# Four heads on separate row and column groups of TensorE, query chunks outermost, in a gated mix of full and dilated attention

## The chip, the cores and the metric

One core of one Trainium2 chip. The metric is the device time of one execution in microseconds (us). The engines are TensorE (PE in the profile; its weight loads are PEld), VectorE (DVE), ScalarE (ACT), GpSimd (POOL) and the DMA queues. Each run is called fast or slow; slow here means more than 1.5% above the fastest run of the same kernel. A burst below is a group of two or three matmuls that start together; a step is the time from one exponential of the main loop to the next.

## The reference, cut to what matters

```python
# B=1, S=2048, D=640, H=32 heads of Dh=20, bf16
g = sigmoid((x * gate_w).sum(-1))
# A: full attention
q, k, v = split(x @ A_wqkv)
a = softmax(q k^T * 20**-0.5) v  @ A_wo            # 32 heads, 2048 x 2048 scores each
# B: each position looks at 8 positions, 2 apart, backwards
b = softmax(q . k[pos - 2w], w = 0..7) v  @ B_wo
return g * a + (1 - g) * b
```

The exponentials of branch A alone are 32 x 2048 x 2048 elements. Spread over 128 partitions that is 1,048,576 columns for ScalarE, whatever the kernel looks like.

## The kernel before

Heads are taken in quads: four heads, each padded to 32 rows, fill 128 partitions. To keep the heads apart, the query tile `qz` is zero outside the rows of one head, and a score matmul contracts all 128 rows. In the value matmul the stationary operand holds the values of all four heads (128 columns), and only one head's rows of the result are used. The loop runs quad, pair, query chunk, key block: 1024 steps.

```python
def mk_qk(s):                       # two heads hh: 128 rows, 20 of them not zero
    for hh in range(2):
        ins = e.matmul(stile[i2][:, hh * 512:(hh + 1) * 512],
                       kTq[bi][:, kb * P:(kb + 1) * P], qz[zb][hh][:, :], start=True, stop=True)
def mk_exp(s):                      # 1024 columns
    e.activation(ebuf[i3][:, :], stile[i2][:, :], ACTF.Exp, scale=SCALE)
def mk_pv(s):                       # all four heads' values, one head's result is used
    for hh in range(2):
        ins = e.matmul(obank[hh][:, :], vAq[bi][:, kb, :],
                       ebuf[i3][:, hh * 512:(hh + 1) * 512], start=(kb == 0), stop=(kb == KBN - 1))
...
for s in range(nsteps):             # 1024 steps
    mk_exp(s); mk_qk(s + 2); mk_pv(s)
    run_side(s, ...)                # projections, branch B, output: one or two matmuls a step
```

Branch B multiplies values by weights and adds them up on VectorE in fp32 (`tmpB`, `blkacc`). Partial outputs of two quads are added to what already lies in HBM: they are read back (`accin`) and written again.

## Time and profile before

| | |
|---|---|
| time | 1508.4 us (median of 4; 1507.1 to 1513.6) |
| TensorE / ScalarE / VectorE busy | 84% / 69% / 55% |
| mean granted TensorE clock | 0.966 |
| exponentials waiting for score tiles | 360.7 us |

The first lines are from the page of the kernel before: busy us by engine (share of the span, instructions), the TensorE clock in 40 slices (tenths of full speed), and the chain of waits by engine.

```profile
PE 1262.1 (84%) x6402; PEld 570.6 (38%) x6528; DVE 832.1 (55%) x1707; ACT 1042.0 (69%) x1037; POOL 98.3 (7%) x176
PEclk8899999999999999998999999989999999999997
PE 67%; DVE 25%; issue 4%; DMA 3%; ACT 1%; another core or an unknown queue 0%; POOL 0%; DVEq 0%; POOLq 0%; ACTq 0%; SPq 0%
```

The page's groups of instructions follow: line, engine, operation, output<-inputs, shapes, count | busy us, mean ns of one | idle time before them and what ended it.

```profile
L598 ACT ACTIVATE ebuf<-stile 128x1024 bf16<-128x1024 f32 x1024 | 1030.8, 1023 | 384.8 <-PE stile L587 360.7
L609 PE MATMUL obank<-ebuf,vAq 128*128 128x512 bf16 x2005 | 610.6, 385 | 53.0 <-DVE rg L634 50.7
L587 PE MATMUL stile<-qz,kTq 128*128 128x512 bf16 x1985 | 608.3, 386 | 7.6 <-ACT ebuf L598 2.6
L871 DVE TENSOR_TENSOR blkacc<-blkacc,tmpB 128x640 f32<-128x640 f32 x112 | 92.4, 825 | 3.8
```

ScalarE's idle time is nearly all spent waiting for score tiles. The timeline of TensorE shows what those wait for (start in us, length, engine, line, operation, count):

```profile
102.28 0.59 PE L609 MATMUL obank<-ebuf,vAq 128*128 128x512 bf16 x2
102.71 0.38 PE L381 MATMUL side<-xT,WkP 128*128 128x512 bf16 x1
102.93 0.59 PE L587 MATMUL stile<-qz,kTq 128*128 128x512 bf16 x2
103.36 0.59 PE L609 MATMUL obank<-ebuf,vAq 128*128 128x512 bf16 x2
```

Read the starts, not the lengths: the lengths overlap. Value matmuls start at 102.28 and again at 103.36, 1.08 us later, with five matmuls in between: 0.216 us each. So a 512-column matmul takes 0.216 us of TensorE at full clock. With two side matmuls a step is 1.30 us. The kernel is bound by the number of matmuls, and most of what each streams is padding.

The 32-row matmul `side<-ones,E` uses another tile mode (32 rows instead of 128):

```profile
105.52 0.59 PE L609 MATMUL obank<-ebuf,vAq 128*128 128x512 bf16 x2
106.05 0.39 PE L381 MATMUL side<-ones,E 32*128 32x512 bf16 x1
106.36 0.11 PEld L587 LDWEIGHTS stile<-qz,kTq 128*128 128x128 bf16 x2 [0.23 <-issue]
```

The second value matmul started at 105.73; the 32-row matmul starts 0.31 us later instead of 0.216, and the next full one again 0.31 us after that. In this trace a change of tile mode costs about 0.1 us.

### The profile page before, as it was taken

How to read it: one execution, taken by the hardware profiler on the slowest of the kernel's cores; microseconds unless marked ns; L12 is line 12 of the kernel's file. 1: busy time of each engine (PE TensorE's matmuls, PEld its weight loads, DVE VectorE, ACT ScalarE, POOL GpSimd, SP SyncE). 2: the span in 40 equal slices, each digit the busy share in tenths (PEclk: the TensorE clock that was granted, in tenths of full speed). 3: DMA queues.
4: the chain of work that ended last, by engine and by line, in shares of the span. 5: the costliest groups of instructions: out<-in, count | busy, mean ns of one | idle time of the engine just before them, and what ended most of it. 6: DMA issues, size and time to landing. Idle time of an engine off the chain costs nothing.

```text
span 1507.6 us, 18855 instructions
## 1 busy us (share of the span) xinstructions
PE 1262.1 (84%) x6402; PEld 570.6 (38%) x6528; DVE 832.1 (55%) x1707; ACT 1042.0 (69%) x1037; POOL 98.3 (7%) x176
## 2 busy tenths in 40 slices
PE   3899988778788988887998889878889888987885
PEld 2444444333333444343443334334334433442332
DVE  7534344578844445688534343448883333456882
ACT  1487786657676787776877668558777656887870
POOL 5111000000100000000000010000000000000012
PEclk8899999999999999998999999989999999999997
DMA  5001000000111000000011111000010111000012
GB/s 204 24 21 38 9 13 10 9 12 13 41 39 33 13 12 15 8 11 12 21 44 36 29 45 32 11 6 14 12 44 24 38 42 42 15 11 12 16 55 74
DMA packets 24588, 43.77 MB, mean 29 GB/s; under 512 B 6929, under 2 KB 14929, under 8 KB 24496
## 3 DMA queue, kind: packets, MB, share of 16 engines
q1 hardware_dynamic: 15376, 17.64, 4.9%
q0 software_dynamic: 7808, 23.28, 4.6%
q10 hardware_dynamic: 1312, 1.64, 0.3%
q8 instruction: 55, 0.90, 0.3%
q14 instruction: 37, 0.30, 0.1%
HBM read 17.04 MB, written 10.49 MB: 18 GB/s over the span
## 4 chain that ended last, share of the span: by engine, by line
PE 67%; DVE 25%; issue 4%; DMA 3%; ACT 1%; another core or an unknown queue 0%; POOL 0%; DVEq 0%; POOLq 0%; ACTq 0%; SPq 0%
PE obank L609 24%; PE stile L587 23%; PE side L381 13%; DVE rg L634 3%; PE side L784 3%; DVE rg L632 3%; DVE tmpB L869 3%; DVE blkacc L871 2%; PE side L464 1%; DMA out_dram<-outsb 1%; PE side L849 1%; DVE oT L639 1%; DVE outsb L693 1%; DVE qTq L450 1%; DVE ident L307 1%
## 5 line engine op out<-in xcount | busy, mean ns | idle before, releaser
L598 ACT ACTIVATE ebuf<-stile 128x1024 bf16<-128x1024 f32 x1024 | 1030.8, 1023 | 384.8 <-PE stile L587 360.7
L609 PE MATMUL obank<-ebuf,vAq 128*128 128x512 bf16 x2005 | 610.6, 385 | 53.0 <-DVE rg L634 50.7
L587 PE MATMUL stile<-qz,kTq 128*128 128x512 bf16 x1985 | 608.3, 386 | 7.6 <-ACT ebuf L598 2.6
L609 PEld LDWEIGHTS obank<-ebuf,vAq 128*128 128x128 bf16 x2048 | 199.5, 99 | 311.8 <-issue 47.4
L587 PEld LDWEIGHTS stile<-qz,kTq 128*128 128x128 bf16 x2048 | 187.2, 99 | 175.4 <-PE stile L587 34.9
L702 POOL DMA_DIRECT2D out_dram<-outsb x64 | 34.7, 543 | 1309.3 <-DVE outsb L693 885.0
L779 DVE TENSOR_TENSOR prod<-qB,kB 128x256 bf16<-128x256 bf16 x320 | 77.2, 286 | 58.6 <-PE side L784 57.3
L784 PE MATMUL side<-prod,Sel 128*128 128x256 bf16 x320 | 71.3, 283 | 42.5 <-DVE prod L779 42.3
L381 PE MATMUL side<-woA_r,oTn 128*128 128x512 bf16 (+1 forms) x252 | 66.2, 309 | 45.6 <-DVE outsb L693 13.0
L632 DVE STREAM_TRANSPOSE rg<-obank 32x512 f32<-32x512 f32 x64 | 45.4, 709 | 97.6 <-PE obank L609 97.2
L871 DVE TENSOR_TENSOR blkacc<-blkacc,tmpB 128x640 f32<-128x640 f32 x112 | 92.4, 825 | 3.8
L693 DVE TENSOR_TENSOR outsb<-side,accin 128x512 bf16<-128x512 f32 x96 | 45.8, 488 | 86.4 <-PE side L381 78.3
L869 DVE TENSOR_TENSOR tmpB<-vB,attnT 128x640 f32<-128x640 bf16 x112 | 91.7, 819 | 1.9
L381 PE MATMUL side<-xT,WqkB 128*128 128x512 bf16 x189 | 72.0, 381 | 10.0 <-DVE qtmp L439 2.9
L419 DVE CAST kTq<-side 128x512 bf16<-128x512 f32 x32 | 22.1, 691 | 89.7 <-PE side L381 89.7
L784 PEld LDWEIGHTS side<-prod,Sel 128*128 128x128 bf16 x320 | 31.6, 100 | 93.5 <-DVE prod L779 60.3
L381 PE MATMUL side<-xT,WqP 128*128 128x512 bf16 x158 | 60.4, 385 | 4.7 <-DVE outsb L697 1.9
L381 PE MATMUL side<-xT,WkP 128*128 128x512 bf16 x159 | 59.7, 393 | 3.3 <-DVE WkP L410 2.9
L381 PEld LDWEIGHTS side<-woA_r,oTn 128*128 128x128 bf16 x256 | 22.9, 98 | 86.7 <-PE side L381 31.7
L646 DVE TENSOR_TENSOR oTn<-oT,Rb 64x512 bf16<-64x512 f32 x64 | 43.6, 682 | 14.1 <-DMA Rb<-oT 13.2
L464 PEld LDWEIGHTS side<-WvA,xT 128*128 128x128 bf16 x640 | 38.5, 103 | 32.6 <-PE stile L587 6.4
L849 PE MATMUL side<-ident,rep 128*128 128x128 bf16 x128 | 22.1, 248 | 32.8 <-DVE rep L844 32.7
(97 smaller groups left out, 818.4 us busy)
## 6 DMA issues: line engine op xcount, KB each, us to landing
out_dram<-outsb POOLq DMA_DIRECT2D x64, 160.0 KB, 2.1
Rb<-oT SPq DMA_DIRECT2D x64, 128.0 KB
accin<-out_dram POOLq DMA_DIRECT2D x48, 160.0 KB, 2.9
qz<-qTq SPq DMA_DIRECT2D x126, 32.0 KB, 1.8
qz<-zbuf SPq DMA_DIRECT2D x60, 32.0 KB, 1.8
WqkA<-in_A_wqkv_dram SPq DMA_DIRECT2D x1, 1600.0 KB, 15.2
WqkB<-in_B_wqkv_dram POOLq DMA_DIRECT2D x1, 1600.0 KB, 7.4
x_tm<-in_A_x_dram SPq DMA_DIRECT2D x1, 960.0 KB
```

What stands on the lines that cost most here:

```text
L381: ins = e.matmul(o, l, r, start=(k == 0), stop=(k == n - 1))
L464: ins = e.matmul(side[sbk][:, i_ * 80:i_ * 80 + 80], xT[:, c, kb * P:(kb + 1) * P], WvA[:, c, 80 * q:80 * q + 80], start=(c == 0), stop=(c ...
L587: ins = e.matmul(stile[i2][:, hh * 512:(hh + 1) * 512], kTq[bi][:, kb * P:(kb + 1) * P], qz[zb][hh][:, :], start=True, stop=True)
L598: return T("act", lambda e: e.activation(ebuf[i3][:, :], stile[i2][:, :], ACTF.Exp, scale=SCALE), reads=[("stile", i2)], writes=[("ebuf", ...
L609: ins = e.matmul(obank[hh][:, :], vAq[bi][:, kb, :], ebuf[i3][:, hh * 512:(hh + 1) * 512], start=(kb == 0), stop=(kb == KBN - 1))
L632: T("dve", lambda e: e.transpose(rg32[32 * sA:32 * sA + 32, :], obank[0][32 * sA:32 * sA + 32, :]), reads=[("obank", 0)], writes=["rgA"])
L634: T("dve", lambda e: e.transpose(rg32[32 * sB:32 * sB + 32, :], obank[1][32 * sB:32 * sB + 32, :]), reads=[("obank", 1)], writes=["rgB"])
L693: T("dve", lambda e, ob=ob, sbk=sbk, c0=c0, c1=c1, r=r: e.tensor_tensor(ob[:, c0:c1], side[sbk][:, 0:c1 - c0], accin[:, r, c0:c1], ALU.add ...
L779: T("dve", lambda e, r=r, f=f, u=u, off=off: e.tensor_tensor(prod[r][:, :], qB[:, f, u * 256:(u + 1) * 256], kB[:, f, off:off + 256], ALU. ...
L784: return e.matmul(side[sbk][:, col:col + 256], Sel4[:, wp, f, :], prod[r][:, :], start=(wp == 0 and f == 0), stop=(wp == 3 and f == CN - 1))
L869: T("dve", lambda e, vv=vv, av=av: e.tensor_tensor(tmpB[:, :, :], vv, av, ALU.mult), reads=[("attnT", ai), "vB4"], writes=["tmpB"])
L871: T("dve", lambda e: e.tensor_tensor(blkacc[:, :, :], blkacc[:, :, :], tmpB[:, :, :], ALU.add), reads=["tmpB"], writes=["blkacc"])
```

## The change

The intent: let the four heads of a quad run side by side. A score matmul takes 32 rows of one head, and four heads sit on four row groups. A value matmul has 21 columns (a column of ones for the denominator, and 20 values) on one of four column groups. Query chunks become the outermost loop, so the output of a chunk is complete and written once; keys and values of all quads stay on chip; branch B is rebuilt so that its sums over the window run on TensorE, with heads along the partitions. The input is transposed by the DMA. A static list scheduler with a cost model now decides where side work goes. The core of the diff (the file is nearly rewritten; the rest is cut):

```diff
-            for hh in range(2):
-                ins = e.matmul(stile[i2][:, hh * 512:(hh + 1) * 512],
-                               kTq[bi][:, kb * P:(kb + 1) * P], qz[zb][hh][:, :], start=True, stop=True)
+            for i in range(n):                        # n = 3, 2, 3, 2, ... units of 512 columns
+                g, r = divmod(u0 + i, 64)
+                kb, j = divmod(r, 4)                  # four heads j of one key block in turn
+                ins = e.matmul(sc[:, i * 512:(i + 1) * 512], kT[32 * j:32 * j + 32, q, kb * P:(kb + 1) * P],
+                               qT[g % 3][32 * j:32 * j + 32, :], start=True, stop=True)
...
-                ins = e.matmul(obank[hh][:, :], vAq[bi][:, kb, :], ebuf[i3][:, hh * 512:(hh + 1) * 512], ...)
+                ins = e.matmul(obank[32 * j:32 * j + DV, :], vA[:, kb, g % NQ, j, :],
+                               ebuf[s % NE][:, i * 512:(i + 1) * 512], start=(kb == 0), stop=(kb == KBN - 1), ...)
...
+        T("pe", 0.26, fn, ...)                        # cost model: a score burst
+    actc = lambda n: 0.18 + n * 0.8334e-3             # cost model: an exponential of n columns
...
+        lim = exps[s - 1].end ...                     # side work may fill TensorE up to here
+        run_side(lim)
```

## The prediction

> **What bounds it now.** TensorE's issue slots. In the timeline from 100 to 107 us every step has two score matmuls, two value matmuls and one side matmul, 0.216 us apart: 1.08 us a step; with two side matmuls, 1.30 us. The page has PE 84% busy and gives it 67% of the chain of waits; the exponentials (ScalarE) sat idle 360.7 us behind the score tiles. Steps average 1.374 us x 1024 = 1407 us, between a first exponential at 61 us and a last at 1467 us. Zero padding wastes the array: 20 of 128 rows are useful in a score matmul.
>
> **What the change does.**
> - Scores: 2048 units of 32 rows, 3 or 2 at once on separate row groups. Values: the same units on separate column groups. 4096 slots (885 us) become two short bursts in each of 820 steps. [...]
> - Cost added: tile-mode switches. [...]around the 32-row matmul side<-ones the next start comes 0.31 us later, not 0.216, on entry and exit: 0.095 us each. Three a step (rows, columns, full) x 820 = about 235 us.
> - Side matmuls: about 1270 slots of 512 columns (projections, dilated branch, output folded once), 275-285 us.
> - PE estimate: [...]about 955 us.
> - Exponentials: the same columns in 820 instructions of 1536 or 1024. Back to back the trace shows starts 0.920 us apart for 1024 columns (0.853 + 0.067), so 874 + 820 x 0.067 = 929 us, plus about 7 us of gate and dilated exponentials. This is the loop's new floor.
> - Removed: the read-back of partial outputs (48 loads), DMA fills of qz and Rb, fp32 accumulation on DVE (blkacc, tmpB: 184 us). DVE falls from 832 to about 430-500 us, off the path.
>
> **Critical path.** ScalarE and TensorE come out nearly equal. The order is static, from a cost model with exponentials 0.11 us too slow[...]. Where side work is dense (projections, dilated branch, at the start of each query chunk) a step should be PE-bound at 1.3-1.5 us; where it has run out, exponential-bound at 1.13 us. I expect a loop of about 1040 us, a first exponential at about 45 us, and a tail of about 22 us.
>
> **Predicted: 1108 us, 8 in 10 between 1035 and 1200.** Faster by over 2%: 0.97; within: 0.02; slower: 0.01.
>
> **Right or wrong.** Right if: exponentials are 85-92% busy and lead the chain, idle mostly behind the score tiles, in dense stretches; score matmuls of one burst start within some 30 ns of each other, and likewise value matmuls; gaps of about 0.1 us follow each change of shape; accin, tmpB, blkacc are gone; DVE under 500 us.
>
> **What would make it wrong.** Column tiles that don't overlap: + 0.3 us a step, total about 1250. [...] PE waiting in order on DVE's evacuations: + 50 to 100 us. Transposing loads slow: first exponential at 70 us or later. The other way, side work spread so evenly that exponentials are never starved: about 1010 us.

TensorE's sum came to about 955 us. What is measured: 0.095 us for a change of tile mode, three times a step, and 275 to 285 us of side matmuls. The total of 1108 us is the sum of the parts: a first exponential at 45 us, a loop of 1040 us and a tail of 22 us. The 0.853 us in the exponentials' floor are 1024 columns at 0.833 ns; in the trace of the changed kernel, 512 columns more take 0.427 us more from start to start (1.330 against 0.903 us), 0.834 ns a column.

## The result, and the profile after

The changed kernel takes 1118.4 us (median of 4 runs, 1110.2 to 1125.1) against 1508.4 us. The ratio is 0.740 (95% interval 0.736 to 0.744). The ratios and intervals here are made from the fast runs of both kernels in the same rounds; they differ from the ratios of the medians by up to 0.003.

The same three lines of the page, of the changed kernel:

```profile
PE 1006.9 (90%) x6213; PEld 306.2 (27%) x6213; DVE 439.5 (39%) x772; ACT 960.8 (86%) x833; POOL 35.7 (3%) x26
PEclk9599998888898989977969997988568998976657
PE 63%; ACT 20%; issue 8%; DVE 6%; ACTq 2%; DMA 1%; DVEq 0%
```

and its groups:

```profile
L743 ACT ACTIVATE ebuf<-score 128x1536 bf16<-128x1536 f32 (+1 forms) x819 | 955.3, 1253 | 98.7 <-PE score L730 93.6
L730 PE MATMUL score<-qT,kT 32*128 32x512 bf16 x2048 | 372.3, 444 | 50.4 <-ACT ebuf L743 45.3
L754 PE MATMUL obank<-ebuf,vA 128*21 128x512 bf16 x2048 | 361.4, 443 | 9.5 <-DVE vA L430 8.8
```

Idle time in front of the exponentials fell from 384.8 to 98.7 us, and the loop now sits near what ScalarE needs. VectorE fell from 832 to 440 us. But the clock line has changed as well: TensorE was granted 0.847 of full speed on average, with whole slices at 5 and 6 tenths, where before it was 0.966. And the chain of waits still leads through TensorE.

The timeline of TensorE at full clock:

```profile
600.26 0.82 PE L368 MATMUL side<-woA_r,oTn 128*128 128x512 bf16 x3
601.01 0.39 PE L730 MATMUL score<-qT,kT 32*128 32x512 bf16 x3
601.33 0.39 PE L754 MATMUL obank<-ebuf,vA 128*21 128x512 bf16 x3
601.66 0.39 PE L368 MATMUL side<-woA_r,oTn 128*128 128x512 bf16 x1
601.98 0.39 PE L730 MATMUL score<-qT,kT 32*128 32x512 bf16 x2
```

Three score matmuls (x3) have the same length as one, 0.39 us: read singly in the trace, they mostly start 3 to 4 ns apart. From the start of a burst to the next tile mode it takes 0.32 us, which is one matmul (0.216) and one change of tile mode (0.10). A step without side work is thus 0.63 us of TensorE, one with side work 0.73 us and the side matmuls.

The same two bursts near the end of the kernel, where no side work is left:

```profile
1069.79 0.61 PE L730 MATMUL score<-qT,kT 32*128 32x512 bf16 x3
1070.33 0.61 PE L754 MATMUL obank<-ebuf,vA 128*21 128x512 bf16 x3
1070.87 0.60 PE L730 MATMUL score<-qT,kT 32*128 32x512 bf16 x2
```

Now it is 0.54 us from burst to burst: matmuls of 512 columns start 0.427 us apart at half clock, and the change of tile mode adds about 0.11 us. The table by stretches (busy us and count of each engine, then the clock) shows the clock at 0.50 in one stretch and 1.00 in one 20 us later:

```profile
500.00:510.00 10.00, 9.90 (x48) 1.82 (x47) 9.51 (x15) 10.00 (x10) 0.00 (x0) 0.50 0.00 0
520.00:530.00 10.00, 9.89 (x65) 3.25 (x62) 3.39 (x8) 9.78 (x10) 0.00 (x0) 1.00 0.01 2
```

TensorE counts as 99% busy in both. The busy share says nothing here; the clock and the number of matmuls do.

**Where the loop's time goes.** Back to back, the shortest distance between two exponentials in this trace is 1.330 us after 1536 columns and 0.903 us after 1024. All 819 at that pace take 914.6 us; that is the loop's floor. I took every exponential's distance to the next above that floor, and sorted it by what TensorE did between the two score bursts, and by its clock at the first of them:

```
steps of the changed kernel      count   time above the floor
full clock, no side work          127        0.9 us
half clock, no side work          131        3.4 us
full clock, side work             465       69.2 us
half clock, side work              95       62.9 us
total                             818      136.4 us   (first exponential at 38.9 us, tail 23.8 us)
```

The tail is what comes after the last exponential. 38.9 + 914.6 + 136.4 + 23.8 = 1113.7 us, which is the span of 1113.9 us but for the last exponential's own excess. So nearly all of the loss lies in steps with side work, and nearly half of it in the 95 of them that ran at half clock. In total the clock was halved for 343 us, in pieces that are multiples of 3.41 us. (The last 1.3 us of this lie after the kernel's end; the figures of the other runs include 1 to 2 us of the same kind.)

### The profile page after: what moved, and what is told of

It is laid out like the page before. It is cut to its first block, busy times and chain, and to the rows that moved or that the text cites. A ratio compares the mean times of both kernels' runs of the same rounds, so it can differ in the third digit from the quotient of the medians.

```text
span 1113.9 us, 15049 instructions
## 1 busy us (share of the span) xinstructions
PE 1006.9 (90%) x6213; PEld 306.2 (27%) x6213; DVE 439.5 (39%) x772; ACT 960.8 (86%) x833; POOL 35.7 (3%) x26
## 4 chain that ended last, share of the span: by engine, by line
PE 63%; ACT 20%; issue 8%; DVE 6%; ACTq 2%; DMA 1%; DVEq 0%
PE side L368 25%; ACT ebuf L743 19%; PE score L730 19%; PE obank L754 18%; ACTq L290 2%; DVE stage L518 2%; DMA xT<-in_A_x_dram 1%; PE side L574 1%; PE side L528 1%; DVE vA L430 1%; DVE kT L387 1%; DVE oTt L455 1%; DVE oNt L466 1%; DVE qabs L410 0%; DVE oTn L469 0%
## 5 line engine op out<-in xcount | busy, mean ns | idle before, releaser
L743 ACT ACTIVATE ebuf<-score 128x1536 bf16<-128x1536 f32 (+1 forms) x819 | 955.3, 1253 | 98.7 <-PE score L730 93.6
L730 PE MATMUL score<-qT,kT 32*128 32x512 bf16 x2048 | 372.3, 444 | 50.4 <-ACT ebuf L743 45.3
L754 PE MATMUL obank<-ebuf,vA 128*21 128x512 bf16 x2048 | 361.4, 443 | 9.5 <-DVE vA L430 8.8
L730 PEld LDWEIGHTS score<-qT,kT 32*128 32x128 bf16 x2048 | 80.5, 93 | 318.7 <-ACT ebuf L743 211.1
L368 PE MATMUL side<-xT,kvw 128*128 128x256 bf16 (+1 forms) x760 | 142.5, 311 | 27.7 <-DMA xT<-in_A_x_dram 26.8
L754 PEld LDWEIGHTS obank<-ebuf,vA 128*21 128x21 bf16 x2048 | 75.0, 90 | 239.5 <-issue 218.2
L368 PEld LDWEIGHTS side<-xT,kvw 128*128 128x128 bf16 x760 | 63.5, 100 | 89.3 <-issue 66.9
L368 PE MATMUL side<-stage,ident 128*128 128x512 bf16 (+1 forms) x192 | 55.6, 395 | 0.0
L586 DVE TENSOR_TENSOR stage<-vB,repB 128x1280 bf16<-128x1280 bf16 x64 | 50.1, 821 | 1.1
L518 DVE TENSOR_TENSOR stage<-qB,kB 128x1280 bf16<-128x1280 bf16 x64 | 48.5, 818 | 0.2
L387 DVE TENSOR_SCALAR kT<-side,onesrow 128x512 bf16<-128x512 f32 x32 | 23.8, 743 | 39.0 <-PE side L368 39.0
```

The source lines that it names most:

```text
L368: ins = e.matmul(o, l, r, start=(first and i == 0), stop=(last and i == n - 1), skip_group_check=True)
L387: t = T("dve", dvc(512), lambda e, b=b, tcc=tcc: e.tensor_scalar(kT[:, q, tcc * 512:(tcc + 1) * 512], side[b][:, :], onesrow[:, 0:1], None ...
L518: T("dve", dvc(CN * TOK, 2), lambda e, w=w, ks=ks: e.tensor_tensor(prodB(w), qB[:, :, :], ks, ALU.mult), reads=["qB", "kB"], writes=[("pro ...
L586: T("dve", dvc(CN * TOK, 2), lambda e, w=w, vs=vs, rr=rr: e.tensor_tensor(prodB(w), vs, rr, ALU.mult), reads=["vB", ("repB", w4)], writes= ...
L730: ins = e.matmul(sc[:, i * 512:(i + 1) * 512], kT[32 * j:32 * j + 32, q, kb * P:(kb + 1) * P], qT[g % 3][32 * j:32 * j + 32, :], start=Tru ...
L743: exps[s] = T("act", actc(512 * n), lambda e: e.activation(ebuf[s % NE][:, 0:512 * n], score[s % 2][:, 0:512 * n], ACTF.Exp, scale=SCALE), ...
```

## The experiments

Theory: two separate causes hold the loop above its floor. First, the static schedule overfills steps, because its cost model knows no changes of tile mode and takes exponentials for slower than they are; TensorE then is the limit there. Second, where side work is thin, TensorE is fed so little that its clock is halved (343 us at a granted clock of 0.50), and the next side work runs at half speed (95 steps, 62.9 us above the floor). Rivals: TensorE waits for VectorE; the half clock is harmless; the gain of the change was not the side-by-side bursts at all.

All ratios in this table are against the kernel before in the same rounds. Half clock and losses are of the profiled run, which for "one more mode change" counts as slow (1227.9 us).

| run | median us | ratio | half clock us | lost: full clock + side | lost: half clock + side |
|---|---|---|---|---|---|
| the changed kernel | 1118.4 | 0.740 | 343 | 69 | 63 |
| four-group fill | 1070.4 | 0.707 | 39 | 77 | 11 |
| one-group fill | 1105.5 | 0.729 | 189 | 75 | 34 |
| one more mode change | 1211.5 | 0.797 | 527 | 87 | 140 |
| one more mode change, with fill | 1137.1 | 0.752 | 114 | 115 | 33 |
| measured costs | 1089.2 | 0.721 | 327 | 15 | 96 |
| measured costs and fill | 1064.6 | 0.703 | 105 | 19 | 51 |
| one column group (wrong result) | 1206.3 | 0.799 | 22 | 216 | 5 |
| one row group | 1980.8 | 1.312 | 1862 | 16 | 828 |
| costs, fill, relieved first group | 1015.2 | 0.672 | 22 | 21 | 1 |
| the same without the fill | 1057.1 | 0.702 | 257 | 17 | 54 |

### The changed kernel once more

> The changed kernel once more, as the base of the other runs on this chip. Expected 1110 to 1125 us and about 340 us at half TensorE clock, as before. If the half-clock time differs much while the time does not, the theory that the clock costs time is in trouble.

This was missed by a little: the median was 1128.3 us, and the profiled run (1128.6 us) was at half clock for 380 us. The four runs took 1110.6, 1128.1, 1128.6 and 1139.0 us, at mean clocks of 0.854, 0.832, 0.832 and 0.820. Only the first counts as fast, so the ratio of the first measurement is used for comparisons. Over all eight runs of this kernel the time rises as the clock falls, from 1110 us at 0.85 to 1139 us at 0.82. That already points to the clock, but it only shows that the two go together.

### Keep the clock up with zero-weight matmuls

```diff
+    def filler(s):                 # only in steps into which no side work was put
+        for j in range(4):
+            ins = e.matmul(obank[32 * j:32 * j + DV, :], zw[:, 0:DV], ebuf[s % NE][:, 0:512],
+                           start=False, stop=False, skip_group_check=True)   # zw is all zero
...
+        n0 = npe()
         run_side(lim)
+        if npe() == n0 and todo and not ended and s < NT:
+            filler(last_e)
```

> In every step without side work (about 260 of 819), four more value matmuls with zero weights, one on each column group, right after the value burst (no further change of tile mode, 0.216 us of TensorE, zeros added to the output bank; the result stays right). Theory [...] the side work that comes next then runs at half clock (63 us of lost exponential time in 95 such steps). Half-clock time falls from 343 to below 80 us and the kernel to about 1065 us (1050 to 1085). Rival: the half clock costs nothing, because those stretches wait for the exponentials: time within 10 us of the changed kernel, whatever the clock does.

It took 1070.4 us, with all four runs within 0.5 us of each other. The clock line of the four-group fill's page:

```profile
PEclk9589999999999999999999999999999999999999
```

Half-clock time fell from 343 to 39 us and the loss in half-clock side steps from 63 to 11 us. The loss at full clock did not move (69 to 77 us). Adding 263 bursts of useless matmuls (1052 matmuls) made the kernel 48 us faster by the medians; all eight runs of the changed kernel (1110 to 1139 us) lie at least 39 us above all four of this one. The rival, that the half clock is harmless, falls.

> The same fill with one column group instead of four: the same TensorE time, a quarter of the array. [...]the share in idle stretches rises only from about 0.23 to 0.28, the clock still halves for over 200 us, and the time stays above 1095 us. Rival: [...]half-clock time and kernel time equal those of the four-group fill.

The run asks what goes with the half clock: the area that is fed, or, as the rival has it, the time in which TensorE runs anything. The shares of fed area, 0.23 and 0.28, are estimates: bursts and fill of 0.216 us on their part of the array, in steps of 1.12 us (the mean of 1.330 and 0.903).

The one-group fill took 1105.5 us, with 189 us at half clock:

```profile
PEclk9699998999998889998969998998989996989758
```

It was meant to keep TensorE busy for exactly as long as the other fill. Its timeline shows that it did not always:

```profile
547.61 0.39 PE L756 MATMUL obank<-ebuf,vA 128*21 128x512 bf16 x3
547.84 0.38 PE L775 MATMUL obank<-ebuf,zw 128*21 128x512 bf16 x1
548.48 0.39 PE L756 MATMUL obank<-ebuf,vA 128*21 128x512 bf16 x2
548.49 0.39 PE L775 MATMUL obank<-ebuf,zw 128*21 128x512 bf16 x1
```

The first fill (`zw`) waits for the value burst and adds 0.216 us; the second falls on a column group that the burst left free, runs at once with it and adds nothing. That was so in 96 of 263 bursts. So this run by itself does not tell fed area from busy time. My number for the half clock (over 200 us) was slightly missed, and in runs further down the fed area does not sort the halvings (146 windows on the wrong side, where 172 fell).

### One more change of tile mode

```diff
     def fn(e):                     # the value burst
+        e.matmul(obank[:, 0:1], zw[:, :], ebuf[s0 % NE][:, 0:1], start=False, stop=False, ...)  # full array, one column
         ins = None
```

> One more change of tile mode in each step: a one-column full-array matmul with zero weights between the score burst and the value burst ([...]the result stays right). Theory: in the about 560 steps that carry side work TensorE is the limit[...]: + 55 to 80 us, about 1185 us; the steps without side work lose next to nothing. Rival: those steps are late because TensorE waits for VectorE's evacuations[...]: less than + 15 us.

It took 1211.5 us, more than expected. What one added change costs was measured in the kernel before: about 0.1 us for the change of mode, and 0.025 us from one one-column full-array matmul to the next, which together give the 0.10 to 0.13 us of the next expectation. But this run mixes two costs, because its half-clock time rose to 527 us. So the same edit was run on top of the four-group fill:

> The extra change of tile mode again, now with the four-group fill, so that the clock stays up (the first run of the extra change also raised the half-clock time from 380 to 527 us, which mixes two costs). Against the fill alone at 1070.4 us: theory, [...]about 520 steps x 0.10 to 0.13 us less what slack they have, + 35 to 65 us. Rival:[...] less than + 10 us.

The theory is that the added change lies on the path where side work is; the rival, that it hides in a wait. The run took 1137.1 us, 67 us above the fill alone, just over the expected range. Here too the excess over the floor was sorted. The steps at full clock with side work account for 38 us of that (77 to 115 us, about 0.07 us for each of some 550 steps). The rest is again clock: half-clock time rose from 39 to 114 us, most of it in the first and the last group of heads. Changes of tile mode are on the path where side work is, and the rival (TensorE waits for VectorE and the added change hides in that wait) falls: it would then have cost less than 10 us.

### Undo the concurrency

Only the order of the units in a group is changed, so that the matmuls of one burst share a row group and a column group. Instructions and counts stay the same, and the result is right. The schedule of side work stays the same but for the first 73 of 819 steps: there the new order asks for the keys and values of all key blocks early, and 36 steps carry other side work.

```diff
-                kb, j = divmod(r, 4)
+                j, kb = divmod(r, KBN)
```

> Undoes the row and column groups' concurrency and nothing else: the units of a group are taken head by head instead of four heads per key block, so that the matmuls of one burst fall on the same row group and the same column group and must run one after another. Same instructions, same counts, same schedule of side work, right result. If the concurrency is what the change gains: a burst of 2 or 3 takes 0.43 or 0.64 us instead of 0.22, a step at least 1.27 us of bursts plus about 0.44 us of side work[...], 1350 to 1450 us in all. Rival: the gain comes from the cheaper dilated branch and the dropped traffic, and bursts were never the point: below 1200 us.

One run of 1420.7 us; three more at 1454 to 1455 us, with a clock of 0.953 instead of 0.981 (the profiled one was at half clock from 32 to 158 us). The timeline of TensorE in the profiled run, in a stretch at full clock:

```profile
599.76 0.81 PE L730 MATMUL score<-qT,kT 32*128 32x512 bf16 x3
600.51 0.82 PE L754 MATMUL obank<-ebuf,vA 128*21 128x512 bf16 x3
601.26 0.39 PE L368 MATMUL side<-woBp,oB 128*128 128x512 bf16 x1
```

A burst of three is now 0.75 us to the next mode instead of 0.32. Everything else that the change brought is still in this kernel, and without the concurrency it is worth 1513.9 - 1420.7 = 93 us, 6% of the time before (median of the same rounds). Letting the bursts run side by side brings another 302 us (1420.7 - 1118.4), or 350 us against the four-group fill, whose clock was also up. Part of this is the first group of heads, where the order of side work differs as well: its steps lost 75 us in the profiled (slow) run and 26 us in the changed kernel. The rival, that the bursts were never the point, falls.

To split rows from columns, one of the two was undone at a time. For the rows, every score matmul reads head 0; for the columns, the key block picks the column group:

```diff
-  kT[32 * j:32 * j + 32, q, ...], qT[g % 3][32 * j:32 * j + 32, :]
+  kT[0:32, q, ...],               qT[g % 3][0:32, :]
```

```diff
-  obank[32 * j:32 * j + DV, :], ... start=(kb == 0), stop=(kb == KBN - 1)
+  obank[32 * (kb // 4):32 * (kb // 4) + DV, :], ... start=(kb % 4 == 0 and j == 0), stop=(kb % 4 == 3 and j == 3)
```

> Wrong result on purpose: every score matmul reads head 0 of its quad, so all fall on row group 0 and a score burst of 2 or 3 runs one after another; the value bursts stay side by side. With both undone the kernel took 1421 us in its fast run, 302 more than the changed kernel. If both halves of the concurrency are worth the same: about + 150 us, 1230 to 1310 us, less if steps have slack for one serial burst but not for two (then below 1230).

> Wrong result on purpose: the column group of a value matmul is chosen by its key block instead of its head, so that the matmuls of one value burst share a column group and run one after another; the score bursts stay side by side. Expected within 30 us of the run with one row group; if the value burst is off the path (nothing waits for it at once), clearly less.

The run with one column group took 1206.3 us, 88 us more than the changed kernel although its clock was up at 0.99, and 136 us more than the four-group fill, whose clock was also up (0.98):

```profile
PEclk9799999999999999999999999999999999999999
```

One row group took 1980.8 us, far outside what I expected, and more than both undone together. Its clock line and its chain of waits say why:

```profile
PEclk8568655555555555555555555555555555555556
PE 97%; DVE 1%; ACTq 1%; DMA 1%; ACT 0%; issue 0%; DVEq 0%
```

The clock fell to half at 216 us and stayed there for 1744 us, although TensorE was 98% busy. My reading, which no run of its own shows, is a trap: with serial score matmuls at half clock ScalarE waits (897 us behind the score tiles), the steps get longer (2.68 us with side work), and rows are fed for a smaller share of a window (0.54, by the count below) than the 0.74 from which the clock came back. So this run does not measure the worth of the row groups; that split stays open. It also passed the comparison with the reference although three heads of every four used the scores of another head. The likely reason is that the softmax is very flat with these inputs (normal numbers times 0.05 give scaled scores of about 0.004, by estimate from the reference). A comparison is thus no proof that a score path is right here.

**What goes with the half clock.** Not the area alone: with both concurrencies undone, a step without side work feeds five matmuls of a quarter of the array, 5 x 0.25 x 0.216 / 1.30 us = 0.21 of the area, and the clock stayed up from 250 to 1431 us; the changed kernel feeds 5 x 0.25 x 0.216 / 1.12 us = 0.24 and was halved. Not busy time: the run with one row group was 98% busy at a mean clock of 0.53. The share of rows fed, whatever the columns, comes closest, as estimates for steps without side work from the 0.216 us of a matmul and the length of a step: 0.3 in the changed kernel and with one row group (both halved), 0.5 with both undone and with the four-group fill, 0.6 with one column group (all three up). The one-group fill has 0.5 as well, but only where its fill did not run at once with the value burst.

A count over all 14 kept traces bears this out. Each trace was cut into the 3.41 us windows of its clock record. A matmul of 512 columns counted for 0.427 us at half clock, the distance of starts measured there, and for half of that, 0.213 us, at full clock (0.216 us from start to start), other widths in proportion, and matmuls that run at once added their rows up to the whole array. Of 3617 windows at full clock, 172 were followed by half clock. I then looked for the one boundary that sorts them best, and counted the windows on its wrong side:

```
share of the window in which      wrong, clock falls    wrong, clock returns
                                  (172 of 3617)         (172 of 1291)
rows are fed                       23 (at 0.37)          55 (at 0.74)
anything streams                   64                   148
columns are fed                   129                   148
area is fed                       146                    81
```

So in these traces the clock fell after a window in which rows were fed for less than about 0.37 of the time, and came back after one with about 0.74 or more. The 20 falls with the one-group fill had 0.23 to 0.38. In the run with one row group the windows that stayed at half clock had 0.54 (median) although something streamed for 0.86 of them. The boundaries are fitted to these traces, some matmul records may be missing, and the return fits least well in the one-group fill (12 of its 20 returns came below 0.74). No run set the share on purpose, so this is the best fit, not a shown cause.

### Measured costs in the scheduler

```diff
-    actc = lambda n: 0.18 + n * 0.8334e-3
+    actc = lambda n: 0.05 + n * 0.8334e-3
-        T("pe", 0.26, ...)                                  # score burst
+        T("pe", 0.216, ..., mode="rows")                    # value burst: mode="cols"; all else: "full"
+                if mode is not None and mode != self.mode:  # on TensorE
+                    dur += 0.1
+            t.end = start + dur + {"pe": 0.09, "act": 0.12, "dve": 0.06}.get(stream, 0.0)
...
+        if s < NT:
+            lim = max(lim, exps[s].end - 0.6)
         run_side(lim)
```

The second part is needed because a step of 0.903 us has 0.63 us of bursts and no room for side work, while the step of 1.330 us has room to spare; the score tiles are double buffered, so one step may run late.

> Only the cost model of the static scheduler is changed, to the durations measured in the changed kernel's trace: exponentials 0.05 us + columns instead of 0.18, 0.1 us at each change of tile mode, the lags of results; and side work may run until 0.6 us before the running exponential ends instead of until the previous one ends. If the losses at full clock (65 to 70 us in steps with side work) come from a schedule that overfills steps: they fall below 40 us. The clock stays an unknown to it. About 1050 us (1020 to 1090). Rival: the total of side work is what costs, wherever it is put: 1110 us or more.

It took 1089.2 us. The loss at full clock fell from 69 to 15 us, as the theory says, and the rival (side work costs the same wherever it is put) falls. The half clock stayed at 327 us and took its own: 96 us, where it was 63. So part of the loss only changed columns in the table; that the loss at full clock stays low when the clock is up is seen in the two versions with fill below (19 and 21 us). The two parts of this edit, costs and limit, were not run apart.

> Both: measured costs in the scheduler and the four-group fill in steps without side work. If the two causes are separate, the gains add up: about 1015 us (1000 to 1040), clock above 0.97. If they are one and the same, no better than the better of the two alone.

It took 1064.6 us, and this expectation was missed. The gains did not add up: 47 of its 74 us of loss lie in the first group of heads, which ran at half clock for 65 us, and its tail grew to 36 us because side work was left over at the end.

### Relieve the first group

This builds on the version with measured costs and fill:

```diff
+    T("pe", 5.0, pe_warm, ...)         # 72 zero matmuls on the score banks while the input arrives
...
-    run_until(("k", 0))
+    for tcc in range(3):               # keys of a part, then values of its four key blocks
+        while not done.get(("kt", 0, tcc)):
+            step(gk, 1e9, True)
+        while not done.get(("v", 4 * tcc + 3, 0)):
+            step(gv, 1e9, True)
...
-            lim = max(lim, exps[s].end - 0.6)
+            lim = max(lim, exps[s].end - 0.57)      # and the fill only where the step has room
```

> Built from what the runs showed: measured costs in the scheduler, fill where the step has room, and the first group of heads relieved: 72 zero matmuls on the score banks warm the clock while the transposed loads arrive, and the value projections of the first 12 key blocks go between the key projections of the prologue instead of into the loop. The first group lost 47 us of exponential time in the version with costs and fill, partly at half clock; that should fall to below 20 us, the tail from 36 to about 24 us: about 1025 us (1010 to 1045). If the first group's loss stays above 35 us, it is not projections and clock that hold it.

It took 1015.2 us (1012.8 to 1016.2), a ratio of 0.672, and its result is right. The parts of this edit were not run apart, but for the fill (next run). The lines of its page:

```profile
PE 947.9 (94%) x7109; PEld 308.3 (30%) x7109; DVE 440.9 (44%) x773; ACT 935.6 (93%) x833; POOL 36.4 (4%) x26
PEclk9999999999999999999999999999999999999999
ACT 64%; PE 19%; issue 13%; DVE 4%; ACTq 0%; DVEq 0%
L769 ACT ACTIVATE ebuf<-score 128x1536 bf16<-128x1536 f32 (+1 forms) x819 | 931.3, 1307 | 13.9 <-PE score L756 13.8
```

Idle time in front of the exponentials is 13.9 us, ScalarE now leads the chain, and the loop is 24 us above its floor of 914.6. The first group lost 3.7 us. The first exponential starts at 42.4 us, 3.6 us later than in the changed kernel, and the tail is 29 us (24 expected).

> The best version (1015.2 us) without the zero fill in the loop; costs, packing and the warmed prologue stay. If the fill is what holds the clock: half-clock time rises from 22 to over 150 us and the time to about 1040 us (1025 to 1060). If a well packed schedule keeps the clock up by itself: within 5 us of 1015.

Without the fill the same kernel takes 1057.1 us, at half clock for 257 us:

```profile
PEclk9999999888668967989889589997895899889959
```

In this kernel the packed schedule does not keep the clock up by itself (257 us at half clock); with the fill it stays up (22 us).

## Why the prediction was right, and where it was not

The prediction of 1108 us (1035 to 1200) held: 1118.4 us. Point by point:

- **The bound before** (TensorE's matmul slots, 0.216 us each) and **the new floor** (exponentials) were right. I gave the floor as 929 us; the trace gives 914.6, because the fixed part of a back-to-back exponential is 0.05 us (0.903 less 1024 columns at 0.834 ns), not 0.067.
- **The three parts of the sum** were close: first exponential at 45 us (38.9 measured), loop 1040 us (about 1050), tail 22 us (23.8). VectorE was put at 430 to 500 us (440), off the path.
- **The mechanism** was right: concurrency is what pays (undone, the kernel is 302 us slower), starts lie 3 to 4 ns apart, a change of tile mode costs 0.1 us, and steps with side work are the slow ones (1.27 us on average at full clock, just under the 1.3 to 1.5 that I said; 1.79 at half clock) while those without run at the exponentials' pace.
- **The length of a burst** (now cut from the prediction) was put too high. A burst takes 0.216 us; with one change of mode it is 0.314. At full clock TensorE's work is 819 x 0.628 + 560 x 0.1 + about 280 = 850 us by this measure, not "about 955 us".
- **The clock was missed altogether.** The prediction took full speed for granted. It was halved for 343 us, and the four-group fill shows what that cost: about 48 us. This error and the one before point in opposite directions, so the total is better than its terms, and that is luck: with the clock kept up by the fill the kernel takes 1070 us, 38 less than I said.
- **"Lead the chain"** was wrong: TensorE leads with 63%, ScalarE has 20%. ScalarE is busy 86% as predicted, but in the dense steps it is TensorE that ends last.
- **What TensorE does in a change of tile mode** is not shown. Each change costs time, 0.10 us at full clock (0.314 us from one burst to the next, less 0.216) and 0.11 us at half clock (0.533 less 0.427). One candidate is the load of the next weights, which also lasts about 0.1 us: within one mode it can start with the matmul before (before the change, at 102.71 for the matmul at 102.93), after a change of mode it starts with its own matmul (both at 601.01 in the changed kernel; the medians lie 1 to 4 ns apart).

## What to carry to other kernels

When heads are narrower than the array, put them on row and column groups, but count the changes of tile mode (0.1 us each here) and put measured durations, not guesses, into a static schedule: fitting side work to the measured slack gained back most of what the steps had lost. Read the granted clock next to the busy share: this kernel became faster and its TensorE clock was then halved for 343 us, and useless matmuls in the idle stretches paid (48 us here, 42 us in the best version). By the best fit here, choose them so that they add to the time in which rows are fed; the one-group fill, which in 96 of 263 bursts ran at once with value matmuls on all rows, left 189 us at half clock, the four-group fill 39. When one idle-time number stops explaining a loss, sort each step's excess over the floor by clock and by what else was in it.
